# Lower parts one third of a block behind their casts, k.v in two copies, six matmuls behind attention's piece, in a float32 attention and feed-forward kernel

## The chip, the cores and the metric

The kernel runs on one core of one Trainium2 chip. Its time is the device time of one execution in microseconds (us). Three runs of the kernel before took 822.28, 823.66 and 825.62 us; the median, 823.66, is the time before. A profiled execution is a run of its own, with its own time.

The core has five engines with an instruction queue each: TensorE (PE; its weight loads are shown as PEld), VectorE (DVE), ScalarE (ACT), GpSimd (POOL) and SyncE (SP), which issues the DMAs here. Each works its queue off in order and waits for the others on semaphores.

## What is computed

For 8 batches of 8 heads of 576 positions of 64 numbers, attention without softmax, a norm by root mean square, and a feed-forward network with SiLU:

```python
kv = np.einsum('bhsd,bhse->bhde', k, v)
out = np.einsum('bhsd,bhde->bhse', q, kv)
rms = np.sqrt(np.mean(out * out, axis=-1, keepdims=True) + 1e-06)
attn = out / rms * g_norm                       # then 4608 tokens of 512
h = x @ w_in                                    # 512 to 2048
g = h * (1.0 / (1.0 + np.exp(-h)))
return g @ w_out                                # 2048 to 512
```

The weights come as 64-bit floats and are turned into float32 on the chip.

## The kernel before

**Upper and lower parts.** TensorE multiplies numbers of a shorter format (float32r) here, so each operand is held as two: an upper part, which ScalarE makes by a cast, and a lower part, which VectorE makes as the operand minus the upper part. A product is then three matmuls: upper by lower, lower by upper, upper by upper. VectorE's subtraction needs ScalarE's cast. Such pairs are: `kh`, `kl` of k.v (L297, L298) and `qh`, `ql` of q (L304, L305) in attention; `make_upper` and `make_lower` (L713, L716) for an operand of the first product; the two halves of `split` in `make_out_sums` (L624, L625) for sums of blocks of w_out; and `gh`, `gl` of the gated numbers (L734, L738).

**Tiles.** The 4608 tokens are nine tiles `t` of 512; d_ff is 16 blocks `f` of 128, and a block has the number g = 16 t + f. Tiles 0 and 1 run block by block: the first product (L509, `products`), SiLU, then the second product into four banks (`project`, L509 too). From tile 2 the first product is done by a scheme of seven smaller products, two blocks in one `pair_step` (tiles 2 to 5) or `seven_step` (tiles 6 to 8); in tiles 6 to 8 the second product too, with sums of w_out's blocks that `make_out_sums` writes to memory (`out_sums`) during tiles 2 to 5.

**A pair step.** Its own seven products (`product`, L724, six matmuls of 256 columns each) come in the order 1, 6 | 2, 7 | 4, 5 | 3. Between them stand the matmuls of the step before's second product (L509): `due` issues a number of `project`s of six matmuls each, two in each of the four gaps in the usual step. Products 1, 2 and 4 and products 6, 7, 5 and 3 share two banks of PSUM: product 2 waits until ScalarE has copied product 1 (L774), product 7 until VectorE has read product 6 (L775), product 4 until ScalarE has copied product 2 (L783), product 5 until VectorE has read product 7 (L784), product 3 until VectorE has read product 5 (L793; L794 behind it reads product 4), and product 6 of the next step until VectorE has read product 3 (L801). L775 also needs L774's copy.

**Jobs in thirds of a block.** All other work is hung on a block's three lists: `first_jobs` (at the start of block g), `mid_jobs` and `last_jobs`. In a pair step of blocks g and g+1 they run so: first(g), products 1 and 6, two `project`s, mid(g), products 2 and 7, two `project`s, last(g), first(g+1), products 4 and 5, two `project`s, mid(g+1), product 3, the remaining `project`s, last(g+1). The functions are recorded in this order, and every engine gets its own instructions in the order of recording; nothing reorders them. So what stands in a list is queued on VectorE ahead of the evacuations of the products that follow.

- `plan(b, g)` puts one batch's attention on the lists. For b from 2: k.v of the four pairs of heads in one bank (`kv_block`, last of g-2), eight copies of 64x64 from the bank to SBUF (`copy_kv`, L292, first of g-1), then for pair c, with s = g + c: `split_q` (mid of s: L304, L305), `split_kv` (last of s: L297, L298), the first half of q by k.v (mid of s+2: L317 to L319), the second half (last of s+2), the sums of squares (last of s+3: L329, L330), and later the norm (L477 to L485, L256 to L258) and the scaling (L337, L345). 320 columns are the second half.
- `make_out_sums(j)` is spread over eight thirds from block 36, 41, 52, 57, 68, 73, 84 and 89 on: two sums of w_out's parts (L618), four combinations (L621), then `split` of one half and `split` of the other in two successive thirds. Both splits use one buffer `both_parts`: cast (L624), subtraction (L625), DMA to `out_sums` (L626). The second cast must wait until the first DMA has read the buffer.
- `prepare` in `pair_step` makes the operands of the next tile in the tile's last step.

In the last gap of a step the code is: `due(len(groups))`, then `prepare(3)`, then `last_jobs` of g+1; so the second half of attention stands behind all remaining matmuls of the second product.

## Time and profile before

| | before |
|---|---|
| median of 3 runs | 823.66 us (822.28 to 825.62) |
| the profiled execution: its time, its span | 822.35 us, 820.3 us |
| busy: PE, PEld | 802.1 us (98%), 792.9 us (97%) |
| busy: DVE, ACT, POOL | 591.4 us (72%), 410.7 us (50%), 112.6 us (14%) |
| DMA | 164.79 MB, 201 GB/s mean |
| granted TensorE clock | 1.00 |

In the profile a matmul's row gives its start and a modelled end, so successive matmuls overlap; how close together they start tells TensorE's pace, and a gap between a modelled end and the next start is idle time. "Idle before, releaser" is how long an engine sat before an instruction and whose semaphore ended that. In a timeline a row merges equal instructions that follow each other: start, length, engine, line, operation, output<-input, count. SPq is SyncE's queue: a row's length there is how long it took until the issue was over, waits included. Tile names are those of the buffers: `hp` a bank of the first product, `gf` and `wi` the scratch in which a pair step gathers its result, `s` the sums of w_out, `at` attention's banks.

### The profile page before, as it was taken

What the parts mean: (1) busy time and instruction counts of PE and PEld (TensorE: products, weight loads), DVE (VectorE), ACT (ScalarE), POOL (GpSimd) and SP (SyncE); (2) the same over time, 40 slices, a digit from 0 to 9 for tenths busy, and PEclk for the clock granted to TensorE, in tenths of its full rate; (3) what the DMA queues carried; (4) which work ended last, traced back from release to release, by engine and by line L of the source; (5) the groups of instructions that cost most, each with busy time, mean ns of one, the idle gap of its engine ahead of it and who ended that gap; (6) DMA issues with size and microseconds to landing.
All of it is one profiled execution on the core that took longest, in us unless ns stands there. A gap on an engine that the chain in (4) does not pass through costs nothing.

```text
span 820.3 us, 18407 instructions
## 1 busy us (share of the span) xinstructions
PE 802.1 (98%) x7340; PEld 792.9 (97%) x7340; DVE 591.4 (72%) x1252; ACT 410.7 (50%) x886; POOL 112.6 (14%) x119
## 2 busy tenths in 40 slices
PE   8999999999999999999999999999999999999997
PEld 7899999999999999999999999999999999999997
DVE  4999946779676677667576766777556887788666
ACT  4887545446534553455435355434443564465443
POOL 2799771322000000000000000000000000000000
PEclk9999999999999999999999999999999999999999
DMA  9993012556377528746565655445687667657653
GB/s 350 413 401 120 1 60 103 206 173 222 108 232 224 194 99 285 218 167 221 197 197 193 236 163 191 172 133 188 201 293 248 206 209 252 229 197 223 214 181 116
DMA packets 76728, 164.79 MB, mean 201 GB/s; under 512 B 7778, under 2 KB 36450, under 8 KB 76642
## 3 DMA queue, kind: packets, MB, share of 16 engines
q1 hardware_dynamic: 76642, 163.61, 58.5%
q8 instruction: 58, 0.95, 0.5%
q14 instruction: 28, 0.23, 0.1%
HBM read 131.07 MB, written 32.51 MB: 199 GB/s over the span
## 4 chain that ended last, share of the span: by engine, by line
PE 80%; DMA 7%; DVE 5%; ACT 4%; issue 2%; POOL 2%; SPq 1%; DVEq 0%; ACTq 0%; POOLq 0%
PE hp L724 29%; PE acc L509 25%; PE hp L509 9%; PE acc L894 8%; PE at L894 4%; DMA wi<-in_moe_w_in 3%; DMA out_sums<-wi 2%; PE hp L894 2%; PE at L284 2%; DMA wi<-sums_in_dram 1%; DMA k<-in_k 1%; ACT gh L734 1%; PE at L317 1%; PE at L319 1%; PE at L318 1%
## 5 line engine op out<-in xcount | busy, mean ns | idle before, releaser
L509 PE MATMUL acc<-wo,gh 128*128 128x256 f32 x1536 | 240.7, 277 | 0.3 <-POOL wo L223 0.3
L509 PEld LDWEIGHTS acc<-wo,gh 128*128 128x128 f32 x1536 | 205.1, 188 | 0.5 <-POOL wo L223 0.5
L724 PE MATMUL hp<-x_second,wi 128*128 128x256 f32 x1152 | 157.1, 279 | 2.0 <-ACT gf L783 1.1
L509 PE MATMUL acc<-wo,gl 128*128 128x256 f32 x768 | 150.2, 277 | 0.0
L724 PEld LDWEIGHTS hp<-x_second,wi 128*128 128x128 f32 x1152 | 143.2, 188 | 3.6 <-ACT gf L783 1.7
L724 PE MATMUL hp<-operand,wi 128*128 128x256 f32 x1008 | 137.0, 279 | 5.5 <-DVE gf L801 2.6
L724 PEld LDWEIGHTS hp<-operand,wi 128*128 128x128 f32 x1008 | 124.8, 188 | 7.9 <-DVE gf L801 3.6
L509 PEld LDWEIGHTS acc<-wo,gl 128*128 128x128 f32 x768 | 116.0, 188 | 0.0
L945 POOL TENSOR_TENSOR e<-e,partial 128x256 f32<-128x256 f32 x2 | 1.5, 730 | 615.7 <-DVE e L945 615.7
L840 ACT ACTIVATE wi<-wi 128x512 f32<-128x512 f32 x48 | 30.4, 633 | 74.3 <-DVE wi L1138 57.3
L734 ACT ACTIVATE gh<-gf 128x512 fp32r<-128x512 f32 x32 | 20.2, 633 | 53.9 <-DVE gf L794 44.3
L734 ACT ACTIVATE gh<-wi 128x512 fp32r<-128x512 f32 x32 | 20.3, 633 | 52.2 <-DVE wi L794 40.1
L509 PE MATMUL hp<-x_second,wi 128*128 128x256 f32 x384 | 46.3, 276 | 0.0
L509 PE MATMUL hp<-x,wi 128*128 128x256 f32 x360 | 44.5, 278 | 0.8 <-POOL x L460 0.8
L509 PEld LDWEIGHTS hp<-x_second,wi 128*128 128x128 f32 x384 | 45.0, 188 | 0.1
L509 PEld LDWEIGHTS hp<-x,wi 128*128 128x128 f32 x360 | 42.4, 188 | 1.2 <-POOL x L460 1.0
L323 ACT ACTIVATE sq<-at 128x256 f32<-128x256 f32 (+1 forms) x56 | 22.8, 408 | 30.0 <-PE at L319 29.9
L894 PE MATMUL acc<-wo,gh 128*128 128x256 f32 x192 | 35.2, 276 | 0.0
L305 DVE TENSOR_TENSOR ql<-q,qh 128x576 fp32r<-128x576 f32 x28 | 22.4, 798 | 16.4 <-ACT qh L304 16.4
L894 PE MATMUL acc<-s,gs 128*128 128x256 f32 x216 | 32.2, 276 | 0.0
L1138 DVE TENSOR_TENSOR wi<-hp,partial 128x256 f32<-128x256 f32 x24 | 10.2, 426 | 30.4 <-PE hp L724 30.4
L530 DVE TENSOR_TENSOR gl<-gf,gh 128x512 fp32r<-128x512 f32 x18 | 13.4, 743 | 23.4 <-ACT gf L529 21.2
(204 smaller groups left out, 1572.0 us busy)
## 6 DMA issues: line engine op xcount, KB each, us to landing
wi<-sums_in_dram SPq DMA_DIRECT2D x112, 512.0 KB, 3.7
s<-out_sums SPq DMA_DIRECT2D x72, 256.0 KB, 4.5
wi<-in_moe_w_in SPq DMA_DIRECT2D x16, 512.0 KB, 8.1
wo<-in_moe_w_out SPq DMA_DIRECT2D x16, 512.0 KB, 9.1
sums_in_dram<-sum_parts SPq DMA_DIRECT2D x16, 512.0 KB, 2.6
out_sums<-wi SPq DMA_DIRECT2D x16, 512.0 KB, 2.9
k<-in_k SPq DMA_DIRECT2D x28, 288.0 KB, 4.9
v<-in_v SPq DMA_DIRECT2D x28, 288.0 KB, 5.3
```

The costliest lines, as they stand in the source:

```text
L284: nc.tensor.matmul(out=self.kv[h], lhsT=self.k[rows, c, :], rhs=self.v[rows, c, :], start=(start and r == 0), stop=(stop and r == 4),)
L305: nc.vector.tensor_tensor(out=self.ql, in0=self.q, in1=self.qh.bitcast(F32), op=ALU.subtract)
L317: nc.tensor.matmul(out=ps, lhsT=self.kh, rhs=self.ql[:, w], start=True, stop=False)
L318: nc.tensor.matmul(out=ps, lhsT=self.kl, rhs=self.qh[:, w], start=False, stop=False)
L323: nc.scalar.activation(out=self.sq[:, self.w], in_=self.ps, func=AF.Square)
L509: nc.tensor.matmul(out=to[:, at:at + 256], lhsT=stationary, rhs=moving[:, at:at + 256], start=start and at == 0, stop=stop and at == n - 256,)
L530: (nc.gpsimd if t == 0 and f >= WARM else nc.vector).tensor_tensor(out=gl, in0=gf, in1=gh.bitcast(F32), op=ALU.subtract)
L724: nc.tensor.matmul(out=out, lhsT=a_of(i, a, c), rhs=x[b][:, c], start=start and n == 0, stop=n == 5, skip_group_check=not check,)
L734: nc.scalar.activation(out=gh, in_=x, func=AF.Silu)
L840: nc.scalar.activation(out=self.gated, in_=self.gated, func=AF.Silu)
L894: nc.tensor.matmul(out=self.out[m], lhsT=g[m], rhs=self.weight(m, j, a), start=j == 0 and n == 0 and m in self.opens, stop=j == HF - 1 and ...
L1138: nc.vector.tensor_tensor(out=first.gated[:, high], in0=u, in1=u3, op=ALU.add)
```

## The change

Four edits; the rest of the program stays as it is.

1. **Lower parts later.** `split_kv` and `split_q` keep the cast alone; the subtractions become `low_kv` and `low_q`. For b from 2 `low_q` goes from mid of s to last of s, `low_kv` from last of s to first of s+1; for b = 1 they stay in their third. In `prepare` the lower parts of one call are made at the next call: `lowers` holds them, one more call stands behind product 5, and the very last one falls into the next step. `make_out_sums` is spread over twelve thirds in place of eight: cast of s23 in the sixth, its subtraction and DMA in the eighth, cast of s41 in the tenth, its subtraction and DMA in the twelfth.
2. **k.v in two copies.** The four `kvm` tiles become one tile, and `copy_kv` for b from 1 copies 64 rows of all four pairs at once (64x4x64, two copies).
3. **The last gap of a pair step.** One `project` (half of what is left), then last of g+1 with attention's second half, then the last `project` of six matmuls.
4. **Order in ScalarE's queue at a tile's end.** `prepare(4, 5)` stands behind the SiLU of the second pair of blocks.

```diff
             nc.scalar.copy(out=self.kh, in_=self.kvm)
+
+        def low_kv(self):
             nc.vector.tensor_tensor(out=self.kl, in0=self.kvm, in1=self.kh.bitcast(F32), op=ALU.subtract)
...
             nc.scalar.copy(out=self.qh, in_=self.q)
+
+        def low_q(self):
             nc.vector.tensor_tensor(
                 out=self.ql, in0=self.q, in1=self.qh.bitcast(F32), op=ALU.subtract
             )
...
-        def split(half, two):
+        def upper(two):
             nc.scalar.copy(out=both_parts[:, 0], in_=two)
+
+        def lower(half, two):
             nc.vector.tensor_tensor(out=both_parts[:, 1], in0=two, in1=both_parts[:, 0].bitcast(F32), op=ALU.subtract)
             nc.sync.dma_start(out=out_sums[j, half], in_=both_parts.bitcast(F32))
...
+            lambda: upper(s23),
             lambda: combine(s41[:, low], s41[:, low], s23[:, low]),
-            lambda: split(0, s23),
-            lambda: split(1, s41),
+            lambda: lower(0, s23),
+            lambda: None,
+            lambda: upper(s41),
+            lambda: None,
+            lambda: lower(1, s41),
...
         def prepare(*ms):
 
+            while lowers:
+                m = lowers.pop(0)
+                make_lower(m, home(m))
             for m in ms if fresh else ():
-                make_operand(m)
+                make_upper(m, home(m))
+                lowers.append(m)
...
         upper_part(c2, hi[0])
+        prepare()
         due(len(groups) // 2)
...
-        prepare(4, 5)
         upper_part(c1, hi[1])
         late_part.append((c1, hi[1], lo[1]))
+        prepare(4, 5)
+        due(len(groups) // 2)
+        run(last_jobs.pop(g + 1, ()))
         due(len(groups))
         prepare(3)
-        run(last_jobs.pop(g + 1, ()))
...
+        def copy_kv():
+
+            bank = banks.pop()[:, :NP * D].rearrange("p (c d) -> p c d", d=D)
+            for h in range(2):
+                d = slice(h * D, (h + 1) * D)
+                nc.scalar.copy(out=all_kvm[d, :, d], in_=bank[d])
...
             at(mid_jobs, s, p.split_q)
-            at(last_jobs, s, p.split_kv)
+            at(last_jobs, s, p.low_q, p.split_kv)
+            at(first_jobs, s + 1, p.low_kv)
...
-            spread_out(lambda j=j: make_out_sums(j), 3 * g, 1, 1, 1, 1, 1, 1, 1, 1)
+            spread_out(lambda j=j: make_out_sums(j), 3 * g, *[1] * 12)
```

Below, lines are those of the kernel before. In the changed kernel the same lines stand a little further down: L298 is L300, L305 is L309, L317 to L319 are L321 to L323, L329 and L330 are L333 and L334, L509 is L513, L618 is L622, L621 is L625, L624 is L628, L625 is L631, L724 is L734, L734 is L744, L738 is L748, L774 is L788, L775 is L789, L783 is L797, L784 is L798, L793 and L794 are L807 and L808, L801 is L816, and the two copies of k.v are L1247.

The order of the instructions is shown at three places, as it was and as it is. The first is VectorE's queue in tile 3 around the step that begins at block 58, with the subtraction for q (`ql`), the evacuation of product 3 (written to `wi`, L801 and now L816) and that of product 6 (L775 and now L789). Before:

```order
L794 TENSOR_TENSOR gf<-hp,wi_3196 128x256
L305 TENSOR_TENSOR ql<-q,qh 128x576
L618 TENSOR_TENSOR s_5103<-wo_1492 128x512
L801 TENSOR_TENSOR wi_3196<-hp,wi_3196 128x256
L738 TENSOR_TENSOR gl<-gf,gh 128x512
L329 STREAM_TRANSPOSE sqT<-sq 128x576
L330 TENSOR_REDUCE sums<-sqT 128x18
L298 TENSOR_TENSOR kl<-kvm_93,kh 128x128
L621 TENSOR_TENSOR s_5103<-s_5103,s_5102 128x256
L621 TENSOR_TENSOR s_5102<-s_5102 128x256
L775 TENSOR_TENSOR wi_3196<-hp,wi_3196 128x256
```

and in the changed kernel:

```order
L808 TENSOR_TENSOR gf<-hp,wi_3172 128x256
L622 TENSOR_TENSOR s_5067<-wo_1480 128x512
L816 TENSOR_TENSOR wi_3172<-hp,wi_3172 128x256
L748 TENSOR_TENSOR gl<-gf,gh 128x512
L333 STREAM_TRANSPOSE sqT<-sq 128x576
L334 TENSOR_REDUCE sums<-sqT 128x18
L309 TENSOR_TENSOR ql<-q,qh 128x576
L625 TENSOR_TENSOR s_5067<-s_5067,s_5066 128x256
L300 TENSOR_TENSOR kl<-kvm,kh 128x128
L625 TENSOR_TENSOR s_5066<-s_5066 128x256
L789 TENSOR_TENSOR wi_3172<-hp,wi_3172 128x256
```

The subtraction for q moved from ahead of product 3's evacuation to behind it; that for k.v moved one combination back.

The second place is VectorE's queue in tile 4 around block 75, with the sums of w_out number 5 (s_6338 and s_6339 before, s_6296 and s_6297 now) and small operations of the norm between them. Before:

```order
L625 TENSOR_TENSOR wi_3506<-s_6338,wi_3506 128x512
L793 TENSOR_TENSOR wi_3196<-hp,wi_3196 128x256
L794 TENSOR_TENSOR wi_3196<-hp,wi_3196 128x256
L256 SCALAR_TENSOR_TENSOR u<-m,y 128x72
L257 SCALAR_TENSOR_TENSOR u<-u,y 128x72
L258 SCALAR_TENSOR_TENSOR y<-u,y 128x72
L625 TENSOR_TENSOR wi_3506<-s_6339,wi_3506 128x512
L801 TENSOR_TENSOR gf<-hp,wi_3196 128x256
```

and in the changed kernel, where the other half's subtraction (L631 of s_6297) follows eleven rows further on:

```order
L807 TENSOR_TENSOR wi_3172<-hp,wi_3172 128x256
L808 TENSOR_TENSOR wi_3172<-hp,wi_3172 128x256
L256 SCALAR_TENSOR_TENSOR u<-m,y 128x72
L257 SCALAR_TENSOR_TENSOR u<-u,y 128x72
L258 SCALAR_TENSOR_TENSOR y<-u,y 128x72
L631 TENSOR_TENSOR wi_3482<-s_6296,wi_3482 128x512
L816 TENSOR_TENSOR gf<-hp,wi_3172 128x256
```

In front of product 3's evacuation now stands the first half's subtraction, whose cast was made two thirds earlier, where the second half's stood.

The third place is ScalarE's queue just behind, at the start of the step of block 76. Before, the second cast stood ahead of the SiLU (L734, L735) of the step before; now it stands behind that, directly ahead of the copy of product 1 (L788):

```order
L628 CAST wi_3482<-s_6297 128x512
L788 COPY wi_3172<-hp 128x256
L797 COPY wi_3172<-hp 128x256
L1247 COPY kvm<-at 64x4x64 x2
L744 ACTIVATE gh<-gf 128x512
```

The same five rows before were:

```order
L624 CAST wi_3506<-s_6339 128x512
L734 ACTIVATE gh<-gf 128x512
L735 ACTIVATE gf<-gf 128x512
L774 COPY wi_3196<-hp 128x256
L783 COPY wi_3196<-hp 128x256
```

The cast moved from ahead of two SiLU operations to the place between them and the copy of product 1.

More of the change, by code (lines that the diff above doesn't have):

```diff
@@ L99, in linear_attention_rms_silu_ffn @@
     gap(gp, 64, "gap_gated")
-    kvm = [const.tile([P, P], F32, name=f"kvm{i}") for i in range(NP)]
-    for t in kvm:
-        nc.gpsimd.memset(t, 0.0)
+    all_kvm = const.tile([P, NP, P], F32, name="kvm")
+    kvm = [all_kvm[:, i] for i in range(NP)]
+    nc.gpsimd.memset(all_kvm.rearrange("p i n -> p (i n)"), 0.0)
     ident = const.tile([P, P], F32, name="ident", tag="kh", bufs=2)
@@ L728, in product @@
                 n += 1
-    late_part = []
+    late_part, lowers = [], []
     def upper_part(x, gh):
@@ L1108, in seven_step @@
             open_gated()
+        while lowers:
+            m = lowers.pop()
+            make_lower(m, home(m))
         slot("")
@@ L1220, in kv_block @@
                 p.mm_kv(chunks=[4], stop=p.c == NP - 1)
+            banks.append(bank)
+        def copy_kv():
[3 more added lines that the diff above has]
+                nc.scalar.copy(out=all_kvm[d, :, d], in_=bank[d])
+        banks = []
         if b > 1:
@@ L1227, in plan @@
                 at(first_jobs, g - 1 + p.c // 3 * 2, lambda p=p: p.load(which="q"))
-                at(first_jobs, g - 1, p.copy_kv)
+            at(first_jobs, g - 1, copy_kv)
         else:
             at(last_jobs, g, kv_block)
-            for p in ps:
-                at(first_jobs, g + 1, p.copy_kv)
+            at(first_jobs, g + 1, copy_kv)
         for p in ps:
@@ L1237, in plan @@
                 split_at, first_at, second_at, sums_at, _ = SECOND[p.c]
-                at_third(split_at, p.split_kv, p.split_q)
+                at_third(split_at, p.split_kv, p.low_kv, p.split_q, p.low_q)
                 at_third(first_at, p.begin_out, half[0])
```

## Prediction

> **What bounds the kernel now.** I read the page first. TensorE's weight loads and matmuls fill the span, and no other engine comes near:
>
> ```profile
> span 820.3 us, 18407 instructions
> PE 802.1 (98%) x7340; PEld 792.9 (97%) x7340; DVE 591.4 (72%) x1252; ACT 410.7 (50%) x886; POOL 112.6 (14%) x119
> ```
>
> So the matmuls set the time, and only TensorE's idle time and its pace can be won. The edits take no matmul away. Next I asked for the busy time by stage, for the stretches from tile 0's middle to tile 2, tiles 2 to 5, and tiles 6 to 8 without the end (columns: stretch, sum, then each engine's busy time, granted clock, DMA share, GB/s):
>
> ```profile
> 60.00:212.00 152.00, 152.00 (x1446) 151.48 (x1445) 121.02 (x218) 82.44 (x181) 71.62 (x63) 1.00 0.36 123
> 212.00:579.00 367.00, 359.74 (x3298) 355.24 (x3297) 250.59 (x526) 171.71 (x384) 0.00 (x0) 1.00 0.58 192
> 579.00:805.00 226.00, 225.75 (x1984) 225.43 (x1982) 163.63 (x401) 109.55 (x221) 0.00 (x0) 1.00 0.69 226
> ```
>
> TensorE has no gap in the first, 0.25 us in the last, and 7.26 us (367.00 less 359.74) in tiles 2 to 5, just where the diff works. Third, the waits from 212 to 606 us, TensorE's own (all of them):
>
> ```profile
> PE hp L724 <- DVE gf L801: 2.6, 3, 1.4
> PE hp L724 <- DVE wi L801: 1.4, 3, 0.6
> PE hp L724 <- ACT gf L783: 1.1, 3, 0.5
> PE hp L724 <- DVE u L256: 0.8, 1, 0.8
> PE hp L724 <- DVE wi L784: 0.7, 1, 0.7
> PE hp L724 <- ACT wi L774: 0.3, 1, 0.3
> PE hp L724 <- DMA wi<-sums_in_dram: 0.3, 1, 0.3
> PE hp L724 <- DVE wi L775: 0.2, 1, 0.2
> ```
>
> All are products that wait for the evacuation of their bank, mostly of product 3 by VectorE (L801), 4.0 us in 6 waits. VectorE is idle a third of this stage, so why is it late? From the same view, what VectorE and ScalarE wait for:
>
> ```profile
> DVE ql L305 <- ACT qh L304: 16.4, 12, 2.5
> DVE wi L793 <- PE hp L724: 14.8, 10, 3.5
> DVE wi L625 <- ACT wi L624: 14.0, 11, 2.6
> DVE kl L298 <- ACT kh L297: 10.3, 8, 1.8
> ```
>
> The row on L793 is the harmless kind, a wait for TensorE's product. In the other three VectorE stands 40.7 us in front of casts, with evacuations queued behind. The timeline at 360 us shows such a stall, on VectorE and then on TensorE (start, length, engine, line, operation; in brackets the idle time before and who ended it):
>
> ```profile
> 359.49 0.76 DVE L305 TENSOR_TENSOR ql<-q,qh 128x576 fp32r<-128x576 f32 x1 [2.53 <-ACT qh L304]
> 360.17 0.69 DVE L618 TENSOR_TENSOR s<-wo 128x512 f32<-128x512 f32 x1
> 360.77 0.42 DVE L801 TENSOR_TENSOR wi<-hp,wi 128x256 f32<-128x256 f32 x1
> ```
>
> ```profile
> 359.77 0.85 PE L724 MATMUL hp<-operand,wi 128*128 128x256 f32 x6
> 361.24 0.97 PE L724 MATMUL hp<-operand,wi 128*128 128x256 f32 x6 [0.62 <-DVE wi L801]
> ```
>
> VectorE sat 2.53 us, did `ql` and a sum, and only then L801, for which TensorE had stopped between products 1 and 6. At 465 us the second cast of `out_sums` itself waits, for the first half's DMA; ScalarE, VectorE and TensorE in turn:
>
> ```profile
> 465.87 0.62 ACT L624 CAST wi<-s 128x512 fp32r<-128x512 f32 x1 [1.26 <-DMA out_sums<-wi]
> ```
>
> ```profile
> 463.67 0.23 DVE L258 SCALAR_TENSOR_TENSOR y<-u,y 128x72 f32<-128x72 f32 x1
> 466.52 0.69 DVE L625 TENSOR_TENSOR wi<-s,wi 128x512 fp32r<-128x512 f32 x1 [2.62 <-ACT wi L624]
> 467.13 0.42 DVE L801 TENSOR_TENSOR gf<-hp,wi 128x256 f32<-128x256 f32 x1
> ```
>
> ```profile
> 465.35 0.87 PE L724 MATMUL hp<-operand,wi 128*128 128x256 f32 x6
> 467.61 0.96 PE L724 MATMUL hp<-operand,wi 128*128 128x256 f32 x6 [1.39 <-DVE gf L801]
> ```
>
> DMA, cast, subtraction, L801, TensorE: one chain, and TensorE's longest wait of all. Last, the pace. In the chain of waits, twelve matmuls take 1.36 us in some stretches and 1.41 us in others:
>
> ```profile
> 223.14 1.36 PE acc L509 x12
> ...
> 293.48 1.41 PE acc L509 x12
> ```
>
> The granted clock is 1.00 in both. Following the chain, the slow pace holds from about 280 to 329, 437 to 465, 537 to 558 and 581 to 600 us, 117 us in all. 0.05 of 1.41 us is 3.5%, so it costs some 4.2 us. Each of these stretches begins behind an interruption of TensorE and ends at another or at a block of k.v.
>
> **The change part by part.** *What a stall costs.* Its idle time, and more: the modelled length of a matmul hides part of it. In the rows at 359.77, six matmuls at 0.113 us apiece take 0.68 us, but the row ends at 0.85, so 0.17 us are gone before idle time counts; and the six behind the stall take 0.97 us, 0.12 more than 0.85, until the matmuls follow each other closely again. So each costs its idle time plus 0.29 us.
>
> *Lower parts behind their casts.* Of the 14 waits I leave out the DMA's 0.3 and the 0.8 put down to L256, a small operation that no product needs; a DMA of the sums is likelier there. Twelve are left, 6.3 us (2.6 + 1.4 + 1.1 + 0.7 + 0.3 + 0.2); with 12 times 0.29 = 3.5 they cost 9.8 us. Which go? At 360 us product 3 was out about 1.8 us before 359.77 (two `project`s and attention's piece, twelve matmuls at 0.113 and three at 0.14), so at 358.0. Without the 2.53 us of waiting, and with `ql` behind it, L801 ends by 358.7; product 6 needs it at 359.77 + 0.68 = 360.45. I take the other waits on L801 to be of this kind. In those on L783 and L774 ScalarE is late, held by that DMA or by a late L801, and L775's follows from the stall at 360. L784's wait, which ends at 424.66, has in VectorE's queue two rows ahead
>
> ```profile
> 422.92 0.75 DVE L305 TENSOR_TENSOR ql<-q,qh 128x576 fp32r<-128x576 f32 x1
> ```
>
> 0.75 us that now come behind L784, against 0.7. So all twelve: -9.8. That is one bound. At the other a third stays, -6.5, because `kl` still follows its cast closely: it moved back by one subtraction of 0.76 us, and its waits are 1.3 each (10.3 in 8).
>
> *The new place of `out_sums`' second cast.* It stands two thirds behind the first half's subtraction, but the last third of one block and the first of the next adjoin, so the distance is one gap between products, 2 to 2.7 us. The rows are: the DMA's median over 16, its longest in the chain, VectorE's last work ahead of the subtraction in the last round, TensorE's product 1 behind it, and ScalarE's copy of a product 1:
>
> ```profile
> out_sums<-wi SPq DMA_DIRECT2D x16, 512.0 KB, 2.9
> ...
> 553.31 3.99 DMA out_sums<-wi
> ...
> 556.07 0.82 DVE L345 SCALAR_TENSOR_TENSOR o<-o,gcol,yT 128x576 f32<-128x576 f32 x1
> ...
> 557.92 0.87 PE L724 MATMUL hp<-operand,wi 128*128 128x256 f32 x6
> ...
> 468.79 0.35 ACT L774 COPY wi<-hp 128x256 f32<-128x256 f32 x1
> ```
>
> In the rounds from blocks 41, 57, 73 and 89 the cast (0.62) now stands on ScalarE directly ahead of product 1's copy (0.35), for which product 2 waits. Product 2 comes 24 matmuls, 2.72 us, behind product 1's start. Round 89: scaling ends at 556.89, subtraction 0.69, DMA 2.9 to 3.99, cast and copy 0.97: 561.45 to 562.54, against 557.92 + 2.72 = 560.64. A stall of 0.8 to 1.9. Round 73: the norm's row ends at 463.90, so 468.46 to 469.55 against 465.35 + 2.72 = 468.07: 0.4 to 1.5. In rounds 41 and 57 neither norm nor scaling stands ahead; with 1.6 us less than round 89 they are 0.8 early at the median and 0.3 late at the longest. In the other four rounds the cast stands ahead of a SiLU, which has a gap to spare. I take the median's 0.8 + 0.4: +1.2, from 0 to +4.0.
>
> The Trainium skill's page "DMA: Bandwidth & Descriptors" (Anatomy of one DMA — SWDGE (gpsimd) path) fits a DMA as 2.0 us plus its bytes over 436 GB/s; for these 512 KB that makes an estimated 3.2 us, 0.3 over the median row, and the sum would be 0.6 higher. The page's fit is for GpSimd's path; the rows, 2.9 and 3.99, lie on both sides of it.
>
> *Two copies of k.v.* Eight cost 1.74 us of ScalarE:
>
> ```profile
> 332.19 1.74 ACT L292 COPY kvm<-at 64x64 f32<-64x64 f32 x8 [4.38 <-PE at L284]
> ```
>
> Two copies of 256 columns are nearest to L774's 0.35, about 0.7 together: one us less for ScalarE, seven times. ScalarE had waited 4.38 us ahead of them, so it isn't what is late: 0, or up to -0.5 in tile 0, where ScalarE is fuller.
>
> *Six matmuls behind attention's piece.* No matmul more or fewer, and product 6 comes as late as before: 0. The operands are two blocks old, and the copies of attention's bank can start 0.68 us (six matmuls) earlier. *Operands at a tile's end*: the casts go behind the SiLU, the subtractions one gap later, with at least one gap to spare: 0, at worst 0.5 at four places.
>
> *The pace.* Fewer stalls begin fewer slow stretches, but also end fewer. I take half: -2.1, from 0 to -4.2.
>
> Sum: -9.8 + 1.2 - 2.1 = -10.7. On the profiled execution's 822.35 (its span and 2 us around it) that is 811.65; the median of the runs, 823.66, lies 1.3 above that execution, so I forecast **813.0 us**. Ends, from the median: -9.8 - 0.5 - 4.2 = -14.5, 809.2; every bad end at once, -6.5 + 4.0 + 2.0 = -0.5, 823.2; one bad end alone, 815 to 816.5, two of them about 818.5.
>
> **The rivals.** *Work, not waits.* VectorE's queue ahead of an evacuation may be too long even without waits. For it: the subtractions only change places. Against it: VectorE is busy 250.59 of 367 us here and stands 40.7 of the rest in front of casts. Then half the gain comes and none of the pace: 823.66 - 4.9 + 1.2 = 820.0; with the pace, 818.
>
> *ScalarE takes over the wait.* The cast that waits for the DMA now blocks product 1's copy. If all four rounds end as late as round 89 can (1.9 each), 7.6 + 4 times 0.29 = 8.8 come back: 823.66 - 9.8 + 8.8 = 822.7. Against it: rounds 41 and 57 have less work ahead.
>
> *The slow pace stays.* If stalls end the slow stretches, a kernel without stalls that falls into one stays in it. From 475 to 805 us, 330 us by 3.5% are 11.6, 7.4 more than the 4.2 now: 823.66 - 8.6 + 7.4 = 822.5. From 212 on, 593 us, 20.8: +16.6, so 831.7, **slower**. It decides from 4.2 + 8.6 = 12.8 us, 366 us of slow pace; slower by 0.5% needs 16.9 us, 483 us. For it: in tiles 6 to 8 TensorE idles 0.25 us in all, so little there would end a stretch. Against it: those tiles ran through at the fast pace (1984 matmuls in 226 us are 0.114 apiece), and in tiles 2 to 5 most of the 14 waits began no slow stretch.
>
> The skill's page "TensorE: Matmul & The Clock Gate" (Wait — 56ns, not 53.3ns?) gives one start-to-start time for a warm array, columns over 2.4 GHz plus 2.5 ns, an estimated 109.2 ns for 256. By that there is one pace: no term of -2.1, so 815.1, and no such rival. The rows show two, 113 and 117.5 ns, so term and rival stay.
>
> **How the numbers follow.** Forecast 0.70; work, not waits 0.13; ScalarE 0.07; slow pace 0.10, of which 0.04 slower. A measurement of this kernel can tell about 0.5%, 4.1 us, from no change, so faster means below 819.5. Nearly all of the forecast (0.69) and most of the first rival (0.11) lie there: 0.80. Slower 0.04, the rest 0.16. The range runs from 808.0, the lower end less a little for the scatter of the runs, to 820.0, where the first rival ends; ScalarE's and the pace's cases, 0.17, stay out.
>
> **What would show it.** In the profile after, the waits of `ql` and of the sums' subtraction for ScalarE, 30.4 us now, should be under 5; TensorE's waits on product 3's evacuation gone; its idle time from 212 us to tile 6 near 2 us in place of 7.26, at the starts of the steps of blocks 76 and 92, on L788. Chain rows of twelve matmuls in 1.41 us would show where the slow pace is. The prediction is wrong if L816 (L801 now) still ends waits of over 1 us in all, if the second cast makes TensorE wait in rounds 41 and 57 too, or if tiles 6 to 8 run at 1.41.

## The result, and the profile after

The changed kernel takes 814.73 us (median of 15 runs, 811.64 to 823.16), the kernel before, beside it, 821.94 (15 runs, 819.23 to 827.66). The ratio is 0.9919 with a 95% interval of 0.989 to 0.9948: faster by 6.7 us (4.3 to 9.0), by more than 0.5% at both ends of the interval. The forecast, 813.0 in a range of 808.0 to 820.0, holds it. The comparisons leave disturbed executions out; of one kernel below, eight_defer_sums, the profiled execution was such a one, and of it only the stretch of tiles 2 to 5 and two counts over all profiles are used.

The page begins so:

```profile
span 812.4 us, 18365 instructions
PE 796.6 (98%) x7340; PEld 789.9 (97%) x7340; DVE 596.2 (73%) x1252; ACT 405.1 (50%) x844; POOL 111.7 (14%) x116
```

Still a kernel of matmuls, 8 us shorter. By stage (columns as before: stretch, sum, busy time of each engine, granted clock, DMA share, GB/s):

```profile
60.00:212.00 152.00, 152.00 (x1426) 151.48 (x1425) 122.48 (x219) 81.29 (x169) 73.46 (x64) 0.98 0.35 122
212.00:579.00 367.00, 366.20 (x3423) 364.42 (x3422) 257.15 (x540) 174.39 (x372) 0.00 (x0) 1.00 0.59 198
```

TensorE's idle time in the second stretch is 0.80 us, where it was 7.26. But the first row has 20 matmuls fewer than before in the same 152 us, and a granted clock of 0.98. Time was won where the prediction looked, and some was lost where it did not look. The starts of three steps in the trace (the first matmul of tile 2's first pair step, of tile 6's first step and of tile 8's last step) cut both executions into four pieces:

| us | before | after | difference |
|---|---|---|---|
| to tile 2 | 212.56 | 218.48 | +5.92 |
| tiles 2 to 5 | 366.35 | 351.66 | -14.69 |
| tiles 6 to 8, to the last step | 221.05 | 221.91 | +0.86 |
| the end | 20.37 | 20.37 | 0 |
| span | 820.3 | 812.4 | -7.9 |

The waits of TensorE from 205 to 600 us, all of them, and under them the largest of VectorE's for ScalarE's casts:

```profile
PE hp L734 <- DMA wi<-sums_in_dram: 1.0, 1, 1.0
PE hp L734 <- ACT wi L788: 0.7, 1, 0.7
```

```profile
DVE wi L789 <- ACT wi L788: 15.3, 13, 3.5
...
DVE kl L300 <- ACT kh L297: 6.8, 6, 1.7
DVE x_second L726 <- ACT x_second L723: 5.1, 4, 1.3
```

No wait on product 3's evacuation (L816) is left. Of the three kinds in which VectorE stood 40.7 us in front of casts, those of `ql` and of the sums' subtraction have no row any more, and `kl` has 6.8 us where it had 10.3. (L789's 15.3 us is no cast but the copy of a product, and no wait of TensorE hangs on it.)

The wait on L788 is the new one, at the step of block 92. ScalarE, then TensorE:

```profile
551.39 0.62 ACT L628 CAST wi<-s 128x512 fp32r<-128x512 f32 x1 [1.27 <-DMA out_sums<-wi]
551.92 0.37 ACT L788 COPY wi<-hp 128x256 f32<-128x256 f32 x1
```

```profile
552.34 0.97 PE L734 MATMUL hp<-operand,wi 128*128 128x256 f32 x6 [0.69 <-ACT wi L788]
```

DMA, second cast, copy of product 1, product 2: the chain that the prediction gave, 0.85 us lost here and 0.22 us at the step of block 76, and nowhere else.

What was lost before tile 2 begins on VectorE at 51 us; GpSimd beside it, then TensorE:

```profile
50.40 0.69 DVE L214 SCALAR_TENSOR_TENSOR full<-wi,conv 128x512 int32<-128x512 int32 x1
51.00 5.62 DVE L300 TENSOR_TENSOR kl<-kvm,kh 128x128 fp32r<-128x128 f32 x1
56.55 0.75 DVE L309 TENSOR_TENSOR ql<-q,qh 128x576 fp32r<-128x576 f32 x1
```

```profile
49.72 1.30 POOL L534 TENSOR_TENSOR gl<-gf,gh 128x512 fp32r<-128x512 f32 x1
50.98 0.62 POOL L189 TENSOR_SCALAR wo_full<-wo_full 128x512 f32<-128x512 f32 x1
51.56 1.29 POOL L223 TENSOR_TENSOR wo<-wo_full,wo 128x512 fp32r<-128x512 f32 x1
...
55.88 0.61 POOL L189 TENSOR_SCALAR wo_full<-wo_full 128x512 f32<-128x512 f32 x1
```

```profile
57.44 0.36 PE L321 MATMUL at<-ql,kh 128*128 128x256 f32 x1 [3.47 <-DVE ql L309]
...
59.88 5.10 PE L513 MATMUL hp<-x,wi 128*128 128x256 f32 x24
```

The same places in the profile of before, again VectorE, GpSimd, TensorE:

```profile
51.61 0.36 DVE L298 TENSOR_TENSOR kl<-kvm,kh 128x128 fp32r<-128x128 f32 x1
```

```profile
50.51 1.31 POOL L530 TENSOR_TENSOR gl<-gf,gh 128x512 fp32r<-128x512 f32 x1
51.78 0.66 POOL L189 TENSOR_SCALAR wo_full<-wo_full 128x512 f32<-128x512 f32 x1
```

```profile
56.16 2.89 PE L509 MATMUL hp<-x,wi 128*128 128x256 f32 x24
```

The first `kl` of batch 1, a subtraction of 128x128 that takes 0.36 us before, is 5.62 us long. It begins as GpSimd's L189 begins, and ends when GpSimd, which works without a pause until 56.49, has no more work. TensorE waits 3.47 us for the `ql` behind it, and then takes 5.10 us for 24 matmuls, which were 2.89 before: the granted clock stands at half,

```profile
58.00:64.00 6.00, 5.26 (x24) 5.09 (x24) 5.86 (x8) 3.89 (x9) 2.53 (x2) 0.50 0.52 209
```

and together this is the +5.9: 3.6 us at the wait, 0.7 in attention's products behind it and 2.2 in the 24 matmuls, less 0.6 by which TensorE was ahead of before until then. The order of the instructions on VectorE is the same there in both kernels.

### The profile page after: what moved, and what is told of

The parts are those of the page before. It is cut to its first block, busy times and chain, and to the rows that moved or that the text cites. A ratio compares the mean times of both kernels' runs of the same rounds, so it can differ in the third digit from the quotient of the medians.

```text
span 812.4 us, 18365 instructions
## 1 busy us (share of the span) xinstructions
PE 796.6 (98%) x7340; PEld 789.9 (97%) x7340; DVE 596.2 (73%) x1252; ACT 405.1 (50%) x844; POOL 111.7 (14%) x116
## 4 chain that ended last, share of the span: by engine, by line
PE 88%; DMA 7%; DVE 2%; issue 1%; ACT 1%; SPq 1%; DVEq 0%
PE hp L734 32%; PE acc L513 29%; PE hp L513 9%; PE acc L910 8%; DMA wo<-in_moe_w_out 4%; PE at L910 4%; PE hp L910 2%; PE at L284 2%; PE at L321 1%; PE at L322 1%; PE at L323 1%; DMA wi<-sums_in_dram 1%; DMA early_wo<-in_q 1%; DMA out_sums<-wi 1%; SPq L273 0%
## 5 line engine op out<-in xcount | busy, mean ns | idle before, releaser
L513 PE MATMUL acc<-wo,gh 128*128 128x256 f32 x1536 | 239.7, 276 | 0.3 <-POOL wo L223 0.3
L513 PEld LDWEIGHTS acc<-wo,gh 128*128 128x128 f32 x1536 | 204.4, 188 | 0.5 <-POOL wo L223 0.5
L734 PE MATMUL hp<-x_second,wi 128*128 128x256 f32 x1152 | 154.8, 277 | 0.0
L513 PE MATMUL acc<-wo,gl 128*128 128x256 f32 x768 | 149.6, 276 | 0.0
L734 PEld LDWEIGHTS hp<-x_second,wi 128*128 128x128 f32 x1152 | 142.0, 188 | 0.3
L734 PE MATMUL hp<-operand,wi 128*128 128x256 f32 x1008 | 133.4, 277 | 1.8 <-DMA wi<-sums_in_dram 1.0
L734 PEld LDWEIGHTS hp<-operand,wi 128*128 128x128 f32 x1008 | 122.9, 188 | 2.6 <-DMA wi<-sums_in_dram 1.2
L513 PEld LDWEIGHTS acc<-wo,gl 128*128 128x128 f32 x768 | 115.7, 188 | 0.0
L513 PE MATMUL hp<-x,wi 128*128 128x256 f32 x360 | 46.7, 287 | 0.8 <-POOL x L464 0.8
L513 PE MATMUL hp<-x_second,wi 128*128 128x256 f32 x384 | 46.3, 276 | 0.0
L513 PEld LDWEIGHTS hp<-x,wi 128*128 128x128 f32 x360 | 44.7, 197 | 1.2 <-POOL x L464 1.0
L744 ACT ACTIVATE gh<-gf 128x512 fp32r<-128x512 f32 x32 | 20.3, 634 | 50.8 <-DVE gf L808 45.2
L513 PEld LDWEIGHTS hp<-x_second,wi 128*128 128x128 f32 x384 | 45.0, 188 | 0.1
L744 ACT ACTIVATE gh<-wi 128x512 fp32r<-128x512 f32 x32 | 20.3, 634 | 37.9 <-DVE wi L808 31.8
L532 ACT ACTIVATE gh<-hp 128x512 fp32r<-128x512 f32 x31 | 18.5, 597 | 29.1 <-PE hp L513 28.9
L534 DVE TENSOR_TENSOR gl<-gf,gh 128x512 fp32r<-128x512 f32 x18 | 13.2, 731 | 24.3 <-ACT gf L533 22.1
```

The source lines that it names most:

```text
L513: nc.tensor.matmul(out=to[:, at:at + 256], lhsT=stationary, rhs=moving[:, at:at + 256], start=start and at == 0, stop=stop and at == n - 256,)
L532: nc.scalar.activation(out=gh, in_=hp[:, :TN], func=AF.Silu)
L534: (nc.gpsimd if t == 0 and f >= WARM else nc.vector).tensor_tensor(out=gl, in0=gf, in1=gh.bitcast(F32), op=ALU.subtract)
L734: nc.tensor.matmul(out=out, lhsT=a_of(i, a, c), rhs=x[b][:, c], start=start and n == 0, stop=n == 5, skip_group_check=not check,)
L744: nc.scalar.activation(out=gh, in_=x, func=AF.Silu)
```

## The experiments

Two questions: what holds `kl` at 51 us, and does the change bring it; and do the two parts of edit 1 each take away the waits that were put down to them. On the way a third came up, the slow pace. "Start" below is the start of tile 2's first pair step, "tiles 2 to 5" and "tiles 6 to 8" are the pieces of the table above.

**The changed kernel again.** No edit.

> The changed kernel as it is. In its profile VectorE's first kl of batch 1 (L300, 128x128) takes 5.62 us at 51.00 us, where GpSimd has work without a pause, TensorE waits 3.47 us for the ql behind it and then runs 7 us at half the granted clock. Theory coincidence: it belongs to the kernel's timing in tile 0, so it is there again, the first pair step of tile 2 starts near 218.5 us, and the time is 813 to 816 us. Rival chance: it belonged to that one execution; kl takes 0.3 to 0.4 us, the step starts near 212.5 and the profiled execution takes about 808 us.

813.11 us (4 runs), ratio 0.9871 (0.9802 to 0.9939). `kl` is 5.67 us long at 50.38, the start is at 217.71, tiles 2 to 5 take 351.49. So it belongs to this kernel and not to one execution. It needn't be in every one: the half clock lowers the mean granted clock, and of the fifteen runs of the first comparison eleven have 0.994 to 0.996, four 0.998 to 1.000.

**Eight copies in the changed kernel.**

```diff
-                nc.scalar.copy(out=all_kvm[d, :, d], in_=bank[d])
+                for c in range(NP):
+                    nc.scalar.copy(out=all_kvm[d, c, d], in_=bank[d, c])
```

> The changed kernel, but copy_kv copies k.v in eight operations again, at the same places. Theory coincidence: the two copies are 1 us shorter on ScalarE, which brought GpSimd 0.2 us forward against VectorE, so that kl came just as a GpSimd operation began; with eight copies kl takes 0.3 to 0.4 us, no 3.5 us wait, no half clock, the first pair step of tile 2 starts near 212.6 and the time is 5 to 6 us below the changed kernel's, about 809. Rival: it comes from another part of the change (the one memset of kvm) or from chance: the long kl stays or comes and goes, step near 218.5, about 814.5. In both cases the stretch from that step to tile 8's last step stays at 573 to 574 us, since the copies were no part of what was late in tiles 2 to 5.

`kl` takes 0.73 us and the start is at 213.38, near what the theory has (0.3 to 0.4, and 212.6). (The eight copies took 1.05 us here, not the 1.73 of before.) But the time is 814.71, no better than with the hold-up (ratio 0.9891, 0.9834 to 0.9948), and the last sentence of the expectation failed: tiles 6 to 8 took 228.54 us. From 600 to 780 us in this kernel, and under it in the changed one:

```profile
600.00:780.00 180.00, 180.00 (x1531) 180.00 (x1530) 131.91 (x321) 85.89 (x173) 0.00 (x0) 1.00 0.66 215
```

```profile
600.00:780.00 180.00, 180.00 (x1591) 180.00 (x1590) 135.69 (x334) 89.09 (x180) 0.00 (x0) 1.00 0.69 223
```

TensorE is busy throughout in both, at a granted clock of 1.00, and does 60 matmuls fewer in one: 117.6 ns apiece against 113.1. This is the slow pace. It begins at 568 us, where 0.21 us pass start to start at tile 6's first step (too little for a row in the view of waits), and nothing ends it until the last step:

```profile
569.65 1.41 PE acc L513 x12
...
700.35 1.41 PE hp L734 x12
```

**Two copies in the kernel before.** Edit 2 alone.

```diff
-    kvm = [const.tile([P, P], F32, name=f"kvm{i}") for i in range(NP)]
-    for t in kvm:
-        nc.gpsimd.memset(t, 0.0)
+    all_kvm = const.tile([P, NP, P], F32, name="kvm")
+    kvm = [all_kvm[:, i] for i in range(NP)]
+    nc.gpsimd.memset(all_kvm.rearrange("p i n -> p (i n)"), 0.0)
...
+        def copy_kv():
+
+            bank = banks.pop()[:, :NP * D].rearrange("p (c d) -> p c d", d=D)
+            for h in range(2):
+                d = slice(h * D, (h + 1) * D)
+                nc.scalar.copy(out=all_kvm[d, :, d], in_=bank[d])
...
```

> The kernel before with edit 2 alone (k.v in two copies, one tile). Theory coincidence: kl of the first pair of batch 1 is caught as in the changed kernel, near 5.6 us long; the first pair step of tile 2 starts near 218.5 in place of 212.6, and the time is 827 to 829. Rival: edit 2 does nothing there, the step starts at 212 to 213, and the time is 821 to 823. The stretch from that step to tile 8's last step (587.4 before) stays within 1.5 us in both.

828.7 us against 821.66, ratio 1.0076 (1.0037 to 1.0115): edit 2 alone makes the kernel slower. `kl` again:

```profile
50.71 5.64 DVE L298 TENSOR_TENSOR kl<-kvm,kh 128x128 fp32r<-128x128 f32 x1
```

The start is at 218.17, tiles 2 to 5 take 365.21. The other executions point the same way: the mean granted clock is 0.993 to 0.997 in nine of the ten and 0.999 in the fastest, 822.33, while twelve of the thirteen of before beside them have 0.997 or more.

**A small operation ahead of `kl`** in the changed kernel.

```diff
-                at_third(split_at, p.split_kv, p.low_kv, p.split_q, p.low_q)
+                nudge = [] if p.c else [lambda p=p: nc.vector.memset(p.kl.bitcast(F32), 0.0)]
+                at_third(split_at, p.split_kv, *nudge, p.low_kv, p.split_q, p.low_q)
```

> The changed kernel with one small VectorE operation more, a memset of the 128x128 buffer of kl directly ahead of the first pair's kl of batch 1, so that kl comes 0.15 to 0.25 us later. Theory coincidence: what catches kl is that it arrives together with the start of a GpSimd operation, so this extra work makes the kernel faster: kl takes 0.3 to 0.8 us, the first pair step of tile 2 starts near 212.8, and the time is about 809. Rival, any arrival: kl waits until GpSimd runs out of work, whenever it arrives; then it is still over 5 us long, and the time 814.5 or more.

`kl` 0.42 us, start at 213.81: one instruction more, and 4.7 us won at the start. The time is not the expected 809 but 814.19 (ratio 0.9883, 0.9825 to 0.994): in the profiled execution, 811.71, the sums' DMA in tile 6 made TensorE wait 1.83 us, and behind that the granted clock stood at 0.50 for 3.4 us; tiles 6 to 8 took 223.69.

**Edit 1 in parts.** First the subtractions for q and k.v alone, in the kernel before:

```diff
...
-            at(last_jobs, s, p.split_kv)
+            at(last_jobs, s, p.low_q, p.split_kv)
+            at(first_jobs, s + 1, p.low_kv)
```

> The kernel before with one part of edit 1 alone: the subtractions for q and k.v of batches 2 and on go one third later; the sums of w_out, the copies of k.v and the last gap stay. Measured by the stretch from tile 2's first pair step to tile 6's first step, 366.35 us before and 351.66 after. Theory separate causes: the eight waits that stand behind ql or kl in VectorE's queue go (those that end at 267, 280, 361, 365, 374, 425, 502 and 517 us of before, 4.7 us), and the slow pace from 280 to 329 with them, so the stretch is 358 to 361 us; the waits at 343, 433, 437, 468, 531, 537 and 559 us stay. Rival one queue: VectorE's waits for the sums' casts keep it late, and little goes without the other part: 363 to 366 us.

813.79 us, ratio 0.9905 (0.9873 to 0.9936): as fast as the whole change, with half its gain in tiles 2 to 5 but no loss at the start (211.74). Tiles 2 to 5 take 359.06, inside the theory's 358 to 361. VectorE's waits for casts, from 205 to 606 us: `ql` has no row, that of the sums stays,

```profile
DVE wi L629 <- ACT wi L628: 18.2, 14, 3.0
...
DVE kl L300 <- ACT kh L297: 6.4, 7, 1.7
```

The list of waits was right only in the main: that at 280 us stayed, and those at 433 and 437, which had been put down to the sums, went. Then the sums alone:

```diff
...
+            lambda: upper(s23),
             lambda: combine(s41[:, low], s41[:, low], s23[:, low]),
-            lambda: split(0, s23),
-            lambda: split(1, s41),
+            lambda: lower(0, s23),
+            lambda: None,
+            lambda: upper(s41),
+            lambda: None,
+            lambda: lower(1, s41),
...
```

> The kernel before with the other part of edit 1 alone: make_out_sums over twelve thirds, casts and subtractions apart; q, k.v, copies and the last gap stay. Theory separate causes: the waits that end at 343, 433, 437, 468, 531, 537 and 559 us of before go (5.0 us) with the slow pace from 437 to 465 and from 537 to 558 (1.9 us), and the two new ones at the starts of the steps of blocks 76 and 92 come (1.1 us): the stretch from tile 2's first pair step to tile 6's first step is 360 to 362 us in place of 366.35; the eight waits behind ql and kl stay. Rival one queue: 364 to 366.

817.65 us, ratio 0.9946 (0.9911 to 0.9981). Tiles 2 to 5 take 360.39, inside 360 to 362, and the mirror image: the sums' wait has no row,

```profile
DVE ql L305 <- ACT qh L304: 17.3, 12, 3.3
...
DVE kl L298 <- ACT kh L297: 10.6, 9, 1.9
```

and the two new waits on the copy of product 1 are there, 0.23 and 0.85 us. The profiled execution ran tiles 6 to 8 at the slow pace, 227.96 us. The parts win 7.3 and 6.0 us in tiles 2 to 5, 13.3 of the change's 14.7: two causes, each worth its own. (Edit 1 whole, with the copies and the tiles of k.v as before, was not run.)

**The last gap alone** (edit 3 in the kernel before).

```diff
-        due(len(groups))
-        prepare(3)
-        run(last_jobs.pop(g + 1, ()))
+        due(len(groups) // 2)
+        run(last_jobs.pop(g + 1, ()))
+        due(len(groups))
+        prepare(3)
```

> The kernel before with edit 3 alone: in the last gap of a pair step one project, attention's second half, then the last project. Theory: it is worth nothing by itself, since what is late is VectorE: the stretch from tile 2's first pair step to tile 6's first step stays at 366.35 us within 1 us, and the time at 821 to 823. Rival: product 6 no longer waits so soon behind attention's copies, and a part of the waits goes: 364 us or less.

Tiles 2 to 5 take 365.47, 0.9 us less, inside the theory's 1 us; the profiles of three kernels that are as before in this stage, but for the copies in one (before itself, two copies, and a small operation more, below) lie between 365.21 and 367.49, so it isn't told from nothing. The time is 828.27 against 822.61, ratio 1.0033 (0.9987 to 1.0079): its ten runs fall into two groups, 821.2 to 822.51 and 827.65 to 830.29, as those of the kernel before beside it do (818.99 to 825.83 and 828.77 to 834.99), and only one of the first was profiled, so what the others lost can't be said.

**No wait at tile 6's first step.** The changed kernel with eight copies, and one cast at the end of tile 5 moved behind the first copy of tile 6:

```diff
...
-        prepare(3)
+        prepare(*(() if t + 1 == OUT7 else (3,)))
+        uppers.extend([3] if fresh and t + 1 == OUT7 else [])
...
+        while uppers:
+            make_upper(uppers[0], home(uppers[0]))
+            lowers.append(uppers.pop())
         while lowers:
```

> The changed kernel with eight copies of k.v, and with the cast for operand 3 at the end of tile 5 moved behind ScalarE's copy of product 1 in tile 6's first step (its subtraction behind that). Without that last edit, this kernel waited 0.21 us at the start of tile 6, fell into the slow pace there (117.8 ns a matmul) and stayed in it for 230 us to the end. Theory pace by interruption: a wait starts it and nothing else, so without the 0.21 us wait tiles 6 to 8 run at 113.3 ns; the stretch from tile 6's first step to tile 8's last, 229.9 us in that kernel, is 221.5 to 223 us, and the time is about 806. Rival: the slow pace belongs to the work of tiles 6 to 8 or to this execution's power and comes anyway: 229 to 231 us, 813 to 815.

The wait is gone, and tiles 6 to 8 take 220.99 us, a little under the theory's 221.5 to 223; one profile does not tell this from chance (see the pace, below). But the time is 811.51 (ratio 0.9885, 0.9849 to 0.9921) and the profiled execution took 815.62, since `kl` was held 5.63 us again, with eight copies: their number does not settle it.

**The second cast one third later**, on top of that.

```diff
-            lambda: upper(s41),
             lambda: None,
+            lambda: upper(s41),
             lambda: lower(1, s41),
```

> As the one before, and the second cast of out_sums goes one third later, behind the copy of product 1 for which it stood in the way (the cast in the eleventh third, its subtraction and DMA in the twelfth as they were). Theory: the waits on L788 at the starts of the steps of blocks 76 and 92 go (0.22 and 0.85 us, and the short slow stretch behind the first), 1.3 us; the stretch from tile 2's first pair step to tile 6's first step is 350.3 us in place of 351.66, and the time 804 to 806. Rival: the subtraction in the twelfth third now waits for the cast, and an evacuation behind it on VectorE comes late: 351.5 to 353.

Tiles 2 to 5 take 350.24 us, as the theory said; both waits on L788 are gone. The time is 813.26 (ratio 0.9878, 0.9831 to 0.9926).

**All of it together**: two copies, the memset ahead of `kl`, the two edits above, and a load of x moved behind the sums' load in tile 6.

```diff
-        between.update({(i, "I"): [lambda i=i: load_quarter(OUT7 + 1, i - 1)] for i in range(1, 5)})
+        between.update({(i, "II"): [lambda i=i: load_quarter(OUT7 + 1, i - 1)] for i in range(1, 5)})
```

> The changed kernel with everything that the runs so far point to: the memset ahead of the first kl of batch 1 (against the hold-up by GpSimd), the cast for operand 3 behind tile 6's first copy, the second cast of out_sums one third later, and in tile 6 the load of a quarter of x behind the load of the sums. Theory: tile 2's first pair step starts near 213.5 us, tiles 2 to 5 take 350.3 us, tiles 6 to 8 to their last step 220 to 222, the end 20.4: 804 to 806 us of span and 806 to 808 of time, below the changed kernel's 814.7. Rival for the rest: the sums' DMA of tile 6 is late all the same and begins a slow stretch, 812 to 816.

The later stages do what was expected or better: 350.45 us for tiles 2 to 5, 219.86 for tiles 6 to 8; from 205 to 800 us the view of TensorE's waits has no row. But in spite of the memset

```profile
50.96 0.17 DVE L1269 MEMSET kl<- 128x128 f32 x1
51.23 5.31 DVE L300 TENSOR_TENSOR kl<-kvm,kh 128x128 fp32r<-128x128 f32 x1
```

`kl` was held: start at 219.60, span 810.3, time 813.32 (12 runs, 807.04 to 821.26), ratio 0.9897 (0.9866 to 0.9928). That is not told apart from the changed kernel. No version here is shown to beat it. The spread points to what the hold-up costs: the five fastest executions of the changed kernel and its variants, 807.04 to 808.18 us, all have a mean granted clock of 0.999, which leaves no room for the half clock behind it.

**A very small operation in the kernel before**, to bring `kl` to the point where it was held elsewhere.

```diff
             nc.scalar.copy(out=self.kh, in_=self.kvm)
+            if (self.b, self.c) == (1, 0):
+                nc.vector.memset(self.kl[:, :1].bitcast(F32), 0.0)
             nc.vector.tensor_tensor(out=self.kl, in0=self.kvm, in1=self.kh.bitcast(F32), op=ALU.subtract)
```

> The kernel before with one very small VectorE operation more, a memset of 128x1 directly ahead of the first kl of batch 1, so that kl comes some 0.2 us later: not 0.20 to 0.24 us before the end of a GpSimd operation, as in three profiles without a hold-up, but at its end, as in the five with one (12 to 43 ns before). Theory coincidence: kl takes about 5.6 us, TensorE waits 3.5 us, and the time is 5 to 7 us above before's. If kl comes 0.1 us or more behind the end, it takes 0.5 to 0.8 us and nothing is lost. Rival: kl is held up only by something that the copies of k.v change besides the time; then it takes under 0.9 us wherever it comes.

It came 25 ns ahead of the end of GpSimd's operation, just where it was aimed, and was not held:

```profile
51.37 0.75 DVE L300 TENSOR_TENSOR kl<-kvm,kh 128x128 fp32r<-128x128 f32 x1
```

So the theory of a coincidence of starts fell, here and in the kernel above. The time, 828.78 in four runs (ratio 1.0109, 1.0063 to 1.0156), is not explained by a hold-up in the profiled execution, 825.19: there the slow pace took some 5.5 us in tiles 2 to 5 (3.7 in that of before).

**Waits put in.** The kernel with all edits, and five memsets ahead of L1120's sum in three steps each of tiles 7 and 8.

```diff
+        for _ in range(5 if t > OUT7 and i % 2 == 0 and i < 6 else 0):
+            nc.vector.memset(u2, 0.0)
         nc.vector.tensor_tensor(out=u2, in0=v, in1=p1, op=ALU.add)
```

> The same, with five VectorE memsets more ahead of the sum behind product 6 in the first, third and fifth step of tiles 7 and 8, which make TensorE wait six times for 0.3 to 0.8 us each, where nothing waited. Theory two paces: behind each wait TensorE goes on at 113.3 or at 117.8 ns a matmul, as it falls, and keeps that pace to the next interruption; so one to five of the six stretches of 19 to 38 us are slow, at 0.7 to 1.5 us each, and the kernel loses 3 to 10 us where the waits alone are 2 to 5. Rival: the waits cost their own length and no more, every stretch at 113.3.

825.96 us, ratio 1.0042 (1.0009 to 1.0075); each wait was longer than planned:

```profile
PE hp L734 <- DVE partial L1123: 9.3, 6, 1.7
```

Tiles 6 to 8 take 236.84 us, 17.0 more than without: 11.0 for six waits, start to start, and 5.9 of slow pace. But the slow pace was there before the first of them, from 569 us, where the view has no wait; it outlasted three of them and ended at the fourth, and behind the other two the pace stayed fast. So a wait can end it, and needn't.

## Why the prediction was right, and where it was wrong

**The waits behind casts: right in cause, too small.** The prediction took 12 waits at 9.8 us. Start to start, the 15 interruptions of tiles 2 to 5 in the profile of before cost 12.7 us, 0.85 each: 9.7 us over the plain pitch (the time from one matmul's start to the next) at the interruption, 0.65 ahead of products that follow attention's longer matmuls, 1.9 where the next gap is two pitches instead of one, 0.4 of slower matmuls after that (each less what the kernel with all edits has in this stage, 350.45 us long). The idle time was read rightly; what comes with it is 0.36 us a wait and not the 0.29 taken from one of them. And the wait of 0.8 us put down to L256, which the sum left out as a DMA's, went too: a DMA's it was (with the subtractions for q and k.v alone, the same product waits 0.67 us and the view names the DMA of the sums), but the sums' new order took it away. So did the small interruptions without idle time.

**The new place of the second cast: right.** Forecast: +1.2, at the starts of the steps of blocks 76 and 92, on L788, nowhere else. Measured: 1.3 with what follows each, at these two places. Moved one third later they were gone, at no cost elsewhere.

**k.v in two copies: the step that failed.** The prediction had 0, or up to -0.5 in tile 0, and excluded a loss by asking what is late. Alone the edit costs 0.76% (0.37 to 1.15); in the profiles, 5.6 us at the start. The copies are 1 us shorter on ScalarE; the cast of w_out behind them comes sooner, and GpSimd, which stood 0.15 us for it in before at 47.4, does not stand any more. ScalarE and GpSimd, before and after:

```profile
44.96 1.73 ACT L292 COPY kvm<-at 64x64 f32<-64x64 f32 x8
...
47.41 1.31 POOL L223 TENSOR_TENSOR wo<-wo_full,wo 128x512 fp32r<-128x512 f32 x1 [0.15 <-ACT wo L222]
```

```profile
44.37 0.73 ACT L1247 COPY kvm<-at 64x256 f32<-64x256 f32 x2
...
46.61 1.30 POOL L223 TENSOR_TENSOR wo<-wo_full,wo 128x512 fp32r<-128x512 f32 x1
```

So GpSimd is 0.2 us ahead against VectorE, and the first `kl` no longer comes while GpSimd does a subtraction (two inputs, L530) but in the last 45 ns of it or in the clamp behind it (one input, L189). Over all 14 profiles, by how long L530 (L532 or L534 elsewhere) still ran when `kl` began:

```
ns left of the subtraction   length of kl, us
+202 +212 +232 +235          0.35  0.36  0.38  0.38
+12 +18 +20 +24 +43          5.62  5.63  5.64  5.66  5.67
+4  +25                      0.73  0.75
-298 -304 -308               5.31  0.42  0.42
```

In all 14 profiles `kl` ends 0.14 to 0.15 us behind the end of a GpSimd instruction, so it is GpSimd that it waits for. Where it comes well inside the subtraction, it runs at its end, four times of four. Where it comes later, it waits for the clamp's end and then runs, four times, or it is passed over until GpSimd is out of work, six times of ten. What decides between these is open. That the edit brings the hold-up is shown by the edit alone, the 0.2 us by these rows; the number of the copies does not decide, since the eight that took 1.05 us left GpSimd no wait either, and that `kl` was free in one such kernel and held in another. The memset ahead of it left it free in two of the three kernels that have it; in one of these, that with waits put in, TensorE waited 2.02 us at the second pair's `ql` instead, and the start was at 216.42.

**Six matmuls behind attention's piece, operands at a tile's end:** forecast 0; the first measured 0.9 us less, not told from 0, the second not tried alone.

**The pace: inside the range, by luck.** -2.1 was half of 4.2, without a reason for the half. In tiles 2 to 5 the slow pace took 3.7 us before and 0.1 after (the matmuls at that pace, times the difference); in tiles 6 to 8 0.7 in both. But the rival that was given 0.10, the slow pace staying, happened in part in other kernels: from tile 6 to the end in the profiled executions with eight copies and with the sums alone, at 8 us. Its reason was half right: over 14 profiles, 106 interruptions over 0.1 us from 205 to 795 us, the slow pace follows 26 of the 77 met at the fast pace and 11 of the 29 met at the slow one, about one in three either way. Each interruption looks like a new draw, and in a kernel with few of them one draw lasts long. Why there are two paces is not settled.

**Tiles 6 to 8.** The 0.3 us left to the DMA of the sums stayed and grew:

```profile
592.69 0.97 PE L734 MATMUL hp<-operand,wi 128*128 128x256 f32 x6 [0.98 <-DMA wi<-sums_in_dram]
```

TensorE comes to it 8.6 us sooner than before, the DMA ends only 7.9 us sooner: a term that was missing, +0.7.

**Work, not waits** is out: TensorE's idle time in the stage fell from 7.26 to 0.80 us with VectorE's work unchanged. **ScalarE takes over the wait** came as far as the two places allowed. In sum, tiles 2 to 5 gave 14.7 us where 10.7 was forecast for all, and the start took back 5.9 that no step had looked for. The time was near the forecast because two errors met, and because the median that it started from lay higher: the forecast was a fall of 10.7 us from 823.66, the measured one is 6.7 (4.3 to 9.0) from 821.94.

## What to carry to other kernels

An in-order engine that waits for another's half of a result makes everything behind it late, even when it is idle a third of the time; look in the waits for what is queued behind such a wait, and put distance between the halves. An edit that only makes an engine off the path faster is not free: follow whom it lets run earlier, and what that one then meets. Where a kernel's executions spread by 2%, compare the pieces of several profiles before the times of two.

## What the runs showed of the hardware

- A VectorE subtraction of 128x128 with both inputs in SBUF took 0.28 us where GpSimd had no work and up to 5.67 us beside GpSimd at work without a pause. Of the Trainium skill, "SBUF — State Buffer" (Who interferes with whom) says that such an instruction contends with a GpSimd instruction that reads SBUF, and that the later of the two is blocked until the earlier is done. The trace agrees for a `ql` that came during L223 (1.85 us in place of 0.75, in the changed kernel with eight copies), but the held `kl` let six GpSimd instructions of at most 1.33 us pass.
- After 3.47 us without a matmul the granted clock was 0.50 from 58 to 64 us. The Trainium skill's page "TensorE: Matmul & The Clock Gate" (What's actually happening) gives half rate after about 3.4 us of idleness. The trace agrees here, but shorter waits were followed by it too: 1.83 us in tile 6 of the kernel with the memset ahead of `kl` and 2.02 us at 59 us in that with waits put in, each with 3.4 us at 0.50 behind it. From 205 us on, waits of up to 1.71 us left the clock at 1.00.
- TensorE has two paces at the same granted clock, 113.3 and 117.8 ns for 256 columns; the slow one held for 228 us without an interruption (the changed kernel with eight copies).
